# Fillers for TensorE, two products on VectorE and a new work list in a fused recurrence and highway kernel

## The chip, the cores and the metric

The kernel runs on one core of one Trainium2 chip. The metric is device time in microseconds (us), the median over several executions. Five executions of the kernel before gave 213.85, 214.18, 214.79, 215.29 and 215.34 us: median 214.79. One execution was taken with the hardware profiler; all durations below come from it.

## What is computed

Inputs are `x` and `f_logit` (4 sequences, 6336 steps, 256 channels, fp32), a `lower_bound` per channel, and two 256x256 weights with a bias. First a gated recurrence along each sequence, then a highway layer on its output:

```python
sig = 1.0 / (1.0 + np.exp(-f_logit))
f = lower_bound + (1.0 - lower_bound) * sig
h = f[:, t] * h + (1.0 - f[:, t]) * x[:, t]        # for each t; y[:, t] = h
H = np.maximum(y @ w_h, 0.0)
T = 1.0 / (1.0 + np.exp(-(y @ w_t + b_t)))
out = T * H + (1.0 - T) * y                        # 25344 tokens x 256, fp32
```

## The kernel before

**Units and pieces.** Work is cut into 25 units. A full unit is 1024 tokens of one sequence, as 8 blocks of 128 tokens; the last unit holds the remaining 192 tokens of each of the four sequences. The recurrence side (the "front") takes a unit in one piece, except the first three, which are cut so that work can begin on small loads: unit 0 gives pieces 0, 1 and 2 (2, 2 and 4 blocks), unit 1 pieces 3 and 4, unit 2 pieces 5 and 6 (4 blocks each). From piece 7 on a piece is mostly a whole unit. The highway side (the "back") takes whole units, except the last.

**One piece, step by step.** Each step has a letter, by which the work list names it.
- L and X: SP loads `f_logit` (tile `lt`) and `x` (tile `xt`), each with 5 buffers (line 106).
- U: ScalarE makes the gate u = sigmoid(-f_logit) in fp16 (L154).
- P: a product bv = u * x in bf16, one operation for two blocks of tokens (128x512), on GpSimd (L160). A piece of 2 blocks has one product, of 4 two, of 8 four.
- A: TensorE transposes u, block by block, into PSUM as uT (L198); F: ScalarE turns uT into the decay f, one operation for each half of the channels (L205).
- B: TensorE transposes bv into PSUM as bT (L215). A and B share two PSUM slots, numbered 0 and 1; the digit behind A or B in the list is the slot.
- S: VectorE's scan along time, y = f * y + bT, one operation for each half of the channels (L230). The factor 1 - lower_bound is left out of y here and put into the weights and matrices behind it.
- Q and W: the two halves of the raw weights are loaded (L125), and VectorE makes the fp16 weights from them in two operations (L148). Each W needs both loads.
- Z and G: TensorE's matmuls on y for the gate (zp) and for the other branch (gp, with y already subtracted through the weights), four of 512 columns for each half of the channels (L245), in three PSUM slots 0 to 2 that O shares.
- T: ScalarE's sigmoid of zp (L251). D: VectorE's d = max(gp, -y') (L256), with y' = (1 - lower_bound) * y, the true recurrence output. E and H: e = d * t, on VectorE (L166), and in part on GpSimd (L160).
- O: TensorE adds y' and e while it transposes them back into token order, two matmuls for each half of the channels of a block (L296 and L297). C and V: ScalarE or VectorE copies the result out of PSUM (L303). R: SP stores it (L309).

**What sets the order.** All of it is written out by hand in one string, `PLAN`. The loop at L365 reads it letter by letter, gives each letter its next piece, and pins each instruction to that order. Each engine carries out its own letters strictly in this order and waits where an operand or a buffer is not ready; so what stands in the list behind a waiting instruction of the same engine waits too. SP issues loads and stores from one queue, in list order.

**VectorE beside GpSimd.** `vector_mul` (L165) records a VectorE product, and the next GpSimd product is made to wait for it (L158 to L163). This is used for e. `EARLY` (L69) lists products of u and x that would go to VectorE through letter p; it is empty.

Of the kernel before, what the change touches and what calls it, by code (L numbers as in the profile page):

```python
# [11 lines left out]
FP32 = mybir.dt.float32  # L12
BF16 = mybir.dt.bfloat16
# [6 lines left out]
def kernel(  # L20
# [16 lines left out]
    nc = tc.nc  # L37
    B, S, D = x.shape
    assert D == 256
    P = 128  # L40
    NH = D // P
    NB = 8
# [23 lines left out]

    LASTQ = 2

    EARLY = []  # L69

# [7 lines left out]
    singles = ctx.enter_context(tc.tile_pool(name="singles", bufs=1))  # L80
# [4 lines left out]
    def new(key, shape, dtype):  # L85
        return pools[key].tile([P, *shape], dtype, tag=key, name=key)

    def pin(ins):
        return tc.keep_in_program_order(ins)
# [12 lines left out]
    def load(i, name, src):  # L102
        u, j0, j1 = fronts[i]
        np_, j = units[u][0], run(fronts[i])
        t = fs[i][name] = new(name, [NB, D], FP32)
        pin(nc.sync.dma_start(t[:np_, :j1 - j0].rearrange("p (k j) d -> p k (j d)", j=j), tokens(src, u, j0, j1, j)))
# [6 lines left out]
    def shape(piece):  # L113

        u, j0, j1 = piece
        return units[u][0], j1 - j0

    lb = singles.tile([P, NH], FP32, name="lb")
    bt = singles.tile([P, NH], FP32, name="bt")
# [4 lines left out]
    def load_weights(k):  # L124
        pin(nc.sync.dma_start(w_raw[:, 1 - k], (moe_w_t, moe_w_h)[k].rearrange("(h p) o -> p h o", p=P)))  # L125
# [25 lines left out]
    def gate(i):  # L151
        np_, nb = shape(fronts[i])
        u = fs[i]["u"] = new("u", [NB, D], FP16)
        pin(nc.scalar.activation(u[:np_, :nb], fs[i]["lt"][:np_, :nb], AF.Sigmoid, scale=-1.0))  # L154
# [13 lines left out]
    def product(i, k, mul):  # L168
        np_, _ = shape(fronts[i])
        if "bv" not in fs[i]:  # L170
            fs[i]["bv"] = new("bv", [NB // 2, D, 2], BF16)
        mul(inner(fs[i]["bv"][:np_, k:k + 1])[:, 0], fs[i]["u"][:np_, 2 * k:2 * k + 2],
            fs[i]["xt"][:np_, 2 * k:2 * k + 2])
# [9 lines left out]
    def psum(slot, shape, key, dtype):  # L183
        tag = ("one" if dtype in (FP16, BF16) else "two") + slot
        return ps1.tile([P, *shape], dtype, tag=tag, name=key)
# [126 lines left out]
    def each(pieces, count):  # L312
        return [(i, k) for i, piece in enumerate(pieces) for k in range(count(piece))]

    def halves_of(pieces):
        return each(pieces, lambda p: len(halves(p)))
# [7 lines left out]
    kinds = {  # L324
        "L": (lambda i, _: load(i, "lt", f_logit), each(fronts, lambda p: 1)),
        "X": (lambda i, _: load(i, "xt", x), each(fronts, lambda p: 1)),
        "Q": (lambda i, k: load_weights(k), [(0, 0), (0, 1)]),
        "U": (lambda i, _: gate(i), each(fronts, lambda p: 1)),
        "P": (lambda i, k: product(i, k, gpsimd_mul), [p for p in products if p not in EARLY]),
        "p": (lambda i, k: product(i, k, vector_mul), [p for p in products if p in EARLY]),  # L330
        "A": (decay_pe, halves_of(fronts)),
        "F": (decay_act, each(fronts, lambda p: NH)),
# [14 lines left out]
    }  # L347

    PLAN = (
        "XLLLXXLXLQQUUA0A1PFFFUFUB0PSSB1A0FFPSSPB1A0XLLXLXXPFUFSSWWPB1A0G0Z1PFFUPSSDPXLLXLB0A1G2Z0PUTFFTPPB1S"  # L350
        "SDUSSEZ1A0G0G2A1DDPFTFFPPZ1A0B1O0O2PSSTFECCUB0Z1B1G0G2SDSDA0Z0TUFTPPPPPPA0G1B1FXLLLXRRXLXDESA0Z0Z2O1"
        "UFTCTB0G0A1O1O2SDPPPFCCB1A0Z1G0O2FTUCB0G1PPPHPSDSEDPA1Z0Z2B0O1FTUCTESA1G0G1B0DDHPPPPSZ2O0O1FUTCCB1SA"
        "0G2Z0B1FDUTPHPPSXXLRLRRRLRXLRRZ1A0G2O0PDTFCEEG1B1A0O2O0UFCCDSG1B0A1Z2Z0SDPHPPPPFTTA1B0O2O1G0HPSFCCZ2"
        "B1A0Z1DUTFTEG0O2PSPLXXRXRRRRDPPHCB1SA0O1G0Z2B1FCUTDEPSG1Z0A0O2FTCPDPPHB1A0Z1G0O2SFTCDEB0Z1A1G0PLLXRR"
        "RRSDPPPUFTO2B0A1Z0G1SHDCFTEO2B0G0Z1A1PPPPCUFTSDHO2B0A1G0Z1SCFTO2B0A1DEPSZ1G0PPPCUFTDHO2B0A1O0G1SCFCD"
        "EZ2B0A1Z0PSTFTPPPG1B1O2A0O0DUCFCSG1Z2A1B0HDELXLLRXRLLRXRRRRRXPSTFPPZ1G0O2B1DTCSZ1G2A0O0PHUFTCDEB1A0G"
        "2Z1O0PSPFTCDPPHB0G1G2A1Z0UFTSA0B1FDEDSPO1O0Z2B0PPCCTPHSO1A1G0Z2B0UFTCDEPSA1G0Z2O1PPDB0FTCSA1Z2G0O1PH"
        "FUCTDELXRRXXRRLRLXXRRRA1B0G0Z1PSFTO2DCB1A0G1Z0O2PPPHSUFCTDEB1A0Z1G2O0PSDFTCB0A1Z1G2SFPPPHDO0B1A0G2ET"
        "UCFPSO1PZ0CDTB1A0Z1G2SFTUHO0A0B1DFG1EPPPPSO2A0CCZ0DFB1O2Z1B0TCUTSESHPPG0A1Z2G1DDRRRRRRRRFFTA1B0O2Z0Z"
        "1FCFSEHTTG2B1G0O1RSDDCO2SRHCZ0G1STRO2TDDEZ0CTERTG1O2O0DVDVCO2CREVO1CRO0RCVRR"  # L360
    )
    assert all(PLAN.count(k) == len(places) for k, (_, places) in kinds.items())
    todo = {k: iter(places) for k, (_, places) in kinds.items()}
    letters = iter(PLAN)
    for k in letters:  # L365
        kinds[k][0](*next(todo[k]), *([next(letters)] if k in "ABZGO" else []))
# [1 line left out]
_INS = ['x', 'f_logit', 'lower_bound', 'moe_w_h', 'moe_w_t', 'moe_b_t']  # L368
# [26 lines left out]
```

## Time and profile before

| | us |
|---|---|
| median of five executions | 214.79 |
| the profiled execution, its own time | 214.18 |
| its span, first to last instruction | 212.3 |
| VectorE (DVE) busy | 195.3 (92%) |
| ScalarE (ACT) busy | 193.7 (91%) |
| TensorE matmuls (PE) busy, with waits inside the pipeline | 187.8 (88%) |
| GpSimd (POOL) busy | 160.9 (76%) |
| data moved by DMA | 78.68 MB, 371 GB/s over the span |

The profile is a page of summaries, and the trace behind it can be asked for stretches of time, for single tiles and for the waits of each engine. A row of a timeline gives start and duration in us, engine, source line, operation, what it writes and reads, its shape, and how many equal instructions follow each other; in brackets stands how long the engine was idle before and what ended that. A duration can overlap that of the next instruction, so a chain is best read from start to start. "Busy" of an engine is an average over stages with different limits: here the ramp at the start, the long middle and the tail must be read apart.

### The profile page before, as it was taken

The page shows a single profiled execution, that of the slowest core. Times are in us where ns is not written, and L with a number is a line of the kernel's source. Part 1 is how long each engine was busy: PE and PEld are TensorE (multiplying, and loading weights), DVE is VectorE, ACT ScalarE, POOL GpSimd, SP SyncE. Part 2 cuts the span into 40 slices and gives each one's busy share as a digit, 9 for nine tenths or more (in the row PEclk, how much of TensorE's full clock was granted, in tenths as well). Part 3 has the DMA queues.
Part 4 walks back from the last instruction along what each step waited for, and adds up shares of the span by engine and source line. Part 5 has one row for each costly group of instructions (what it writes and reads, how often), then busy time and mean ns, then how long its engine had stood idle before and what let it go on. Part 6 is the DMA issues. An engine that isn't in the chain of part 4 may idle for free.

```text
span 212.3 us, 4616 instructions
## 1 busy us (share of the span) xinstructions
PE 187.8 (88%) x1800; PEld 131.3 (62%) x1800; DVE 195.3 (92%) x154; ACT 193.7 (91%) x194; POOL 160.9 (76%) x133
## 2 busy tenths in 40 slices
PE   0368998899898999999999999999999999999970
PEld 0255564577575757666767666668576676866770
DVE  1269999999999999999999999999999999999980
ACT  2757999999999999999999999999999999998760
POOL 4485756979599698978988898898899876866400
PEclk9999999999999999999999999999999999999999
DMA  4999999999999999999999999999999996252465
GB/s 96 392 414 426 428 429 421 429 420 420 429 421 424 421 424 421 425 424 418 431 417 421 428 431 420 419 414 431 414 429 412 357 406 269 98 201 99 198 259 188
DMA packets 17349, 78.68 MB, mean 371 GB/s; under 512 B 2352, under 2 KB 2864, under 8 KB 11952
## 3 DMA queue, kind: packets, MB, share of 16 engines
q1 hardware_dynamic: 16784, 78.39, 90.3%
q8 instruction: 14, 0.23, 0.4%
q10 hardware_dynamic: 544, 0.00, 0.1%
q14 instruction: 7, 0.06, 0.1%
HBM read 52.43 MB, written 25.95 MB: 369 GB/s over the span
## 4 chain that ended last, share of the span: by engine, by line
DMA 32%; PE 27%; ACT 21%; DVE 8%; issue 7%; POOL 1%; SPq 1%; ACTq 1%; DVEq 0%; POOLq 0%
DMA xt<-in_x_dram 12%; DMA lt<-in_f_logit_dram 12%; DMA out_dram<-o 8%; PE zp L245 8%; ACT t L251 7%; PE gp L245 6%; ACT u L154 5%; ACT f L205 5%; ACT o L303 4%; DVE d L256 4%; PE uT L198 4%; PE op L296 3%; PE op L297 3%; PE bT L215 3%; DVE y L230 3%
## 5 line engine op out<-in xcount | busy, mean ns | idle before, releaser
L160 POOL TENSOR_TENSOR bv<-u,xt 128x512 bf16<-128x512 f16 (+1 forms) x100 | 114.6, 1180 | 31.5 <-DVE e L166 14.1
L230 DVE TENSOR_TENSOR_SCAN y<-f,y,bT 128x1024 bf16<-128x1024 f16 (+3 forms) x56 | 106.3, 1916 | 2.1 <-PE bT L215 2.1
L205 ACT ACTIVATE f<-uT,ncc 128x1024 f16<-128x1024 f16 (+3 forms) x60 | 65.0, 1095 | 2.5 <-PE uT L198 2.5
L251 ACT ACTIVATE t<-zp,bt 128x1024 bf16<-128x1024 f32 (+1 forms) x52 | 62.9, 1228 | 0.3 <-DVE e L166 0.3
L256 DVE SCALAR_TENSOR_TENSOR d<-y,ncc,gp 128x1024 bf16<-128x1024 bf16 (+1 forms) x52 | 62.3, 1208 | 0.4 <-issue 0.2
L245 PEld LDWEIGHTS <-w_sb 128*128 128x128 f16 x400 | 37.8, 98 | 37.3 <-issue 5.7
L303 ACT COPY o<-op 128x1024 f32<-128x1024 f32 (+2 forms) x50 | 54.9, 1137 | 4.2 <-PE op L297 2.1
L154 ACT ACTIVATE u<-lt 128x2048 f16<-128x2048 f32 (+3 forms) x30 | 52.7, 1759 | 5.1 <-DMA lt<-in_f_logit_dram 5.1
L245 PE MATMUL gp<-y,w_sb 128*128 128x512 bf16 (+1 forms) x200 | 51.4, 382 | 0.7 <-ACT t L251 0.4
L245 PE MATMUL zp<-y,w_sb 128*128 128x512 bf16 (+1 forms) x200 | 50.6, 377 | 0.9 <-DVE d L256 0.6
L296 PE MATMUL op<-diag,y 128*128 128x128 f16 (+1 forms) x400 | 49.2, 219 | 1.8 <-DVE d L256 0.7
L160 POOL TENSOR_TENSOR e<-d,t 128x1024 bf16<-128x1024 bf16 x21 | 44.8, 2135 | 7.3 <-DVE e L166 2.6
L297 PE MATMUL op<-ident_b,e 128*128 128x128 bf16 (+1 forms) x400 | 49.2, 219 | 0.0
L297 PEld LDWEIGHTS <-e 128*128 128x128 bf16 (+1 forms) x400 | 44.7, 114 | 5.5 <-issue 3.3
L296 PEld LDWEIGHTS <-y 128*128 128x128 bf16 (+1 forms) x400 | 44.8, 114 | 2.7
L198 PE MATMUL uT<-ident_h,u 128*128 128x128 f16 (+1 forms) x400 | 32.1, 226 | 9.9 <-ACT u L154 7.4
L198 PEld LDWEIGHTS <-u 128*128 128x128 f16 (+1 forms) x400 | 27.3, 101 | 17.1 <-ACT u L154 7.6
L215 PE MATMUL bT<-ident_f,bv 128*128 128x128 f32 (+1 forms) x200 | 32.5, 284 | 5.2 <-DVE y L230 2.4
L215 PEld LDWEIGHTS bT<-ident_f,bv 128*128 128x128 f32 (+1 forms) x200 | 22.8, 145 | 12.1 <-issue 4.1
L166 DVE TENSOR_TENSOR e<-d,t 128x1024 bf16<-128x1024 bf16 (+2 forms) x26 | 18.9, 734 | 0.1
L230 DVE TENSOR_TENSOR_SCAN y<-f,bT 128x512 bf16<-128x512 f16 (+2 forms) x8 | 10.4, 1335 | 3.9 <-PE bT L215 3.9
L135 DVE TENSOR_SCALAR cc<-lb 128x2 f32<-128x2 f32 x1 | 0.2, 170 | 4.5 <-DMA lb<-in_lower_bound_dram 4.5
(19 smaller groups left out, 10.9 us busy)
## 6 DMA issues: line engine op xcount, KB each, us to landing
out_dram<-o SPq DMA_DIRECT2D x48, 512.0 KB, 13.6
lt<-in_f_logit_dram SPq DMA_DIRECT2D x21, 1024.0 KB, 14.7
xt<-in_x_dram SPq DMA_DIRECT2D x21, 1024.0 KB, 15.8
lt<-in_f_logit_dram SPq DMA_DIRECT2D x5, 512.0 KB, 8.1
xt<-in_x_dram SPq DMA_DIRECT2D x5, 512.0 KB, 8.2
lt<-in_f_logit_dram SPq DMA_DIRECT2D x2, 384.0 KB, 13.0
xt<-in_x_dram SPq DMA_DIRECT2D x2, 384.0 KB, 11.3
xt<-in_x_dram SPq DMA_DIRECT2D x2, 256.0 KB, 5.1
```

The source lines that it names most:

```text
L154: pin(nc.scalar.activation(u[:np_, :nb], fs[i]["lt"][:np_, :nb], AF.Sigmoid, scale=-1.0))
L160: ins = pin(nc.gpsimd.tensor_mul(out_, a, b))
L198: pin(nc.tensor.transpose(uT[:, j * np_:(j + 1) * np_], fs[i]["u"][:np_, j, h * P:(h + 1) * P], ident_h[:np_, :np_]))
L205: pin(nc.scalar.activation(f[:, :N].rearrange("p (k q j) -> p k q j", q=np_, j=j), fs[i]["uT", h].rearrange("p (k j q) -> p k q j", q=np_, ...
L215: pin(nc.tensor.transpose(t[:, k // r, k % r], fs[i]["bv"][:np_, k, h * P:(h + 1) * P].rearrange("p d j -> p (d j)").bitcast(FP32), ident_ ...
L230: pin(nc.vector.tensor_tensor_scan(y, fs[i]["f", h][:, c:c + w], fs[i]["bT", h][:, c:c + w], 0.0 if prev is None else prev, op0=ALU.mult, ...
L245: pin(nc.tensor.matmul(p[:, a:e], w_sb[:, k, ki, h * P:(h + 1) * P], y_of(j)[:, ki, a:e], start=ki == 0, stop=ki == NH - 1))
L251: pin(nc.scalar.activation(bs[j]["t"][:, m, :width(backs[j])], bs[j]["zp", m], AF.Sigmoid, bias=bt[:, m:m + 1]))
L256: pin(nc.vector.scalar_tensor_tensor(bs[j]["d"][:, m, :width(backs[j])], y_of(j)[:, m], ncc[:, m:m + 1], bs[j]["gp", m], op0=ALU.mult, op1 ...
L296: pin(nc.tensor.matmul(o, y[:, h, cols], diag[:, h], start=True, stop=False))
L297: pin(nc.tensor.matmul(o, bs[j]["e"][:, h, cols], ident_b, start=False, stop=True))
L303: pin(copy(bs[j]["o", q][:np_, a:e], bs[j]["op", q][:np_, a:e]))
```

## The change

Three things change.

1. A tile `filler` of zeros is made by VectorE at the very start, and a letter M is added: one TensorE matmul of 512 columns of these zeros with themselves, into a PSUM tile `busy` in slot 2 that nobody reads. The new list has 20 of them: nine ahead of the first transposes, one between the transposes of pieces 0 and 1, one ahead of piece 0's B, seven behind it and ahead of piece 2's A, one ahead of piece 1's B and one ahead of piece 2's.
2. `EARLY` names the product of piece 0 and the first of piece 2's two. VectorE makes these (letter p): the first ahead of all scans, the second between the scans of piece 0's two halves. GpSimd makes two products fewer.
3. `PLAN` is another list. Its ramp loads f_logit of pieces 0 and 1 first, then x of both, f_logit and x of piece 2, one half of the weights, f_logit and x of piece 3, the other half of the weights, and f_logit of piece 4; before it was x of piece 0, f_logit of 0, 1 and 2, x of 1 and 2, f_logit and x of 3, f_logit of 4, and both weight halves. VectorE's order in the ramp was S S S S S S W W S S D S S D and is p S p S S S S W S W S S D D S S. Later on the letters are the same in number, and many neighbours and slots are exchanged.

```diff
-    EARLY = []
+    EARLY = [(0, 0), (2, 0)]
...
+    filler = singles.tile([P, 512], BF16, name="filler")
+    nc.vector.memset(filler, 0.0)
...
     PLAN = (
-        "XLLLXXLXLQQUUA0A1PFFFUFUB0PSSB1A0FFPSSPB1A0XLLXLXXPFUFSSWWPB1A0G0Z1PFFUPSSDPXLLXLB0A1G2Z0PUTFFTPPB1S"
-        "SDUSSEZ1A0G0G2A1DDPFTFFPPZ1A0B1O0O2PSSTFECCUB0Z1B1G0G2SDSDA0Z0TUFTPPPPPPA0G1B1FXLLLXRRXLXDESA0Z0Z2O1"
...
+        "LLXXLXQLXUUMMMMMMMMMA0MA1pFFFUFMB0PSpSMMMMMMMA1MB0FFUSSPMB1A0QLLXLXLXXPFFUSWSWPB0A1Z0G1PUFUFTPSSDPLL"
+        "XXLG2B0A1Z1PFFTPPB1DSSUSSEZ2A0G0G1A1DDPFTFFPPZ2B0A1O0O1PSSTFCUCEB1Z2G0B0G1SDSDA1Z0UTFTPPPPPPA1G2B0FX"
...
     )
...
+    busy = psum("2", [NB * P], "busy", FP32)
     letters = iter(PLAN)
     for k in letters:
+        if k == "M":
+            pin(nc.tensor.matmul(busy[:, :512], filler[:, :P], filler, start=True, stop=True))
+            continue
         kinds[k][0](*next(todo[k]), *([next(letters)] if k in "ABZGO" else []))
```

More of the change, by code (lines that the diff above doesn't have):

```diff
@@ L349 @@
     PLAN = (
-        "XLLLXXLXLQQUUA0A1PFFFUFUB0PSSB1A0FFPSSPB1A0XLLXLXXPFUFSSWWPB1A0G0Z1PFFUPSSDPXLLXLB0A1G2Z0PUTFFTPPB1S"
-        "SDUSSEZ1A0G0G2A1DDPFTFFPPZ1A0B1O0O2PSSTFECCUB0Z1B1G0G2SDSDA0Z0TUFTPPPPPPA0G1B1FXLLLXRRXLXDESA0Z0Z2O1"
-        "UFTCTB0G0A1O1O2SDPPPFCCB1A0Z1G0O2FTUCB0G1PPPHPSDSEDPA1Z0Z2B0O1FTUCTESA1G0G1B0DDHPPPPSZ2O0O1FUTCCB1SA"
-        "0G2Z0B1FDUTPHPPSXXLRLRRRLRXLRRZ1A0G2O0PDTFCEEG1B1A0O2O0UFCCDSG1B0A1Z2Z0SDPHPPPPFTTA1B0O2O1G0HPSFCCZ2"
-        "B1A0Z1DUTFTEG0O2PSPLXXRXRRRRDPPHCB1SA0O1G0Z2B1FCUTDEPSG1Z0A0O2FTCPDPPHB1A0Z1G0O2SFTCDEB0Z1A1G0PLLXRR"
@@ L355 @@
[L355 to L359, printed above, removed]
@@ L360 @@
-        "1FCFSEHTTG2B1G0O1RSDDCO2SRHCZ0G1STRO2TDDEZ0CTERTG1O2O0DVDVCO2CREVO1CRO0RCVRR"
+        "LLXXLXQLXUUMMMMMMMMMA0MA1pFFFUFMB0PSpSMMMMMMMA1MB0FFUSSPMB1A0QLLXLXLXXPFFUSWSWPB0A1Z0G1PUFUFTPSSDPLL"
+        "XXLG2B0A1Z1PFFTPPB1DSSUSSEZ2A0G0G1A1DDPFTFFPPZ2B0A1O0O1PSSTFCUCEB1Z2G0B0G1SDSDA1Z0UTFTPPPPPPA1G2B0FX"
+        "RLLXLLRXXDESA1Z0Z1O2UFTCTB1G0A0O2O1SDPPPFCCB0A1Z2G0O1FTUCB1G2PPHPPSDSEDPA0Z0Z1B1O2FTTUCESG0A0G1B1DDH"
+        "PPPPPSO2O0Z1FUCTCB0SA1G2Z1B0FDUTHPPSLLRRRRRXXXRRLLLZ0G2A1O1PDTFCEEG0B0O2A1O1UFCCDSG0B1A0Z2Z1SDHPPPPP"
@@ new lines @@
+        "FTTB0A1O2O0G1HPSFCCB1Z2Z0A0DUTFTEG1O2PSPRXDPPHCB1SA0Z0G1O2B1FUTCDEPSA0G1Z0O2FTCPDPPHB1A0Z1G0O2SFTCDE"
+        "B0A1Z1G0O2PXRXRRRLRXXRLRRSDPPPUFTB0A1Z0G1SHDCFTEO2B1Z0G1A0PPPPCUFTSDHO2B1A0Z1G0SCFTO2B1A0DEPSZ1G0PPP"
+        "CFTUDHB0O2O1A1G0SCFCDEZ2B0A1Z1PSTFTPPG0O2A1B0O1DCFCUSG2Z0Z1B1A0PHDELLRRRLXXRLXRRLRRPSTFPPG2O0A0B1DTF"
+        "CUSO1G2Z0PHCTDEA0B1Z2G1O0PSPFTCDPPHB0A1Z2G1FTUSG0B1A0FDEDSPO2O1Z0B0PPCCTPHSO2A1G1Z0B0UFCTDEPSA1Z1G2O"
+        "0PPPDB0TFCSZ1A1G2O0HUFCTDERXXRRRRRLLXXRLRXB0A1Z2G0PSFTO1DCB1A0O2G0Z1PPPHSUFTCDEB1A0Z0G1O2PSDFTCB0A1G"
@@ L361 @@
+        "0SFPPHDO1B1A0Z2G0EUCTFPPSO1PZ2CDTB0A1Z1G0SFTUHO2A1B0DFG1EPPPPSO0A1CCZ2DFB0Z0O1B1TUCTSESHPPG2A0Z1G0DD"
+        "RRRRRRRRFFTB0A1O1Z2Z0FFCSEHTTG1G2B1O0RSDDCO1SRHCZ2G0STRO1TDDEZ2CTERTG0O1O2DCVDO1CVREVO0CRO2RCVRR"
     )
+    assert set(PLAN) <= {*kinds, *"M012"}
     assert all(PLAN.count(k) == len(places) for k, (_, places) in kinds.items())
     todo = {k: iter(places) for k, (_, places) in kinds.items()}
+    busy = psum("2", [NB * P], "busy", FP32)
     letters = iter(PLAN)
     for k in letters:
+        if k == "M":
+            pin(nc.tensor.matmul(busy[:, :512], filler[:, :P], filler, start=True, stop=True))
+            continue
```

## The prediction

> **What bounds the kernel now.** I read the page's busy times first, then the busy time by stretches, then the stretch before full load instruction by instruction.
>
> ```profile
> PE 187.8 (88%) x1800; PEld 131.3 (62%) x1800; DVE 195.3 (92%) x154; ACT 193.7 (91%) x194; POOL 160.9 (76%) x133
> ```
>
> Two engines are almost full. The stretches (start:end, length, then PE, PEld, DVE, ACT, POOL busy, clock, DMA share, GB/s) show that they are full from about 15 us to 190 us and that only the two ends have room:
>
> ```profile
> 10.00:15.00 5.00, 3.63 (x22) 2.77 (x22) 3.18 (x5) 2.63 (x5) 4.68 (x5) 1.00 1.04 410
> 15.00:20.00 5.00, 3.39 (x16) 2.31 (x17) 5.00 (x6) 3.62 (x6) 3.11 (x3) 1.00 1.04 425
> 80.00:100.00 20.00, 19.48 (x194) 13.71 (x192) 19.73 (x15) 20.00 (x20) 17.33 (x14) 1.00 1.01 422
> 100.00:120.00 20.00, 19.45 (x202) 13.98 (x199) 20.00 (x13) 20.00 (x19) 18.37 (x15) 1.00 1.02 424
> ```
>
> So the end of the kernel is set by how far VectorE has come when it becomes full, plus what it loses later. Later losses are small: 40 to 140 us show 19.90, 19.74, 19.73, 20.00 and 19.92 of 20, together 0.7 us. The chain that ended last names loads over its first 70 us; but from 15 us on no wait for a load holds VectorE or ScalarE, so I read those shares as DMA being busy alongside. VectorE's own timeline in the ramp:
>
> ```profile
> 9.53 1.26 DVE L230 TENSOR_TENSOR_SCAN y<-f,bT 128x256 bf16<-128x256 f16 x2 [3.92 <-PE bT L215]
> 11.30 1.39 DVE L230 TENSOR_TENSOR_SCAN y<-f,y,bT 128x256 bf16<-128x256 f16 x2 [0.50 <-PE bT L215]
> 14.01 2.45 DVE L230 TENSOR_TENSOR_SCAN y<-f,y,bT 128x512 bf16<-128x512 f16 x2 [1.32 <-PE bT L215]
> 16.38 2.30 DVE L148 SCALAR_TENSOR_TENSOR w_sb<-o,cc 128x512 f16<-128x512 f32 x2
> 18.60 2.32 DVE L230 TENSOR_TENSOR_SCAN y<-f,bT 128x512 bf16<-128x512 f16 x2
> 20.84 1.25 DVE L256 SCALAR_TENSOR_TENSOR d<-y,ncc,gp 128x1024 bf16<-128x1024 bf16 x1
> ```
>
> The number to beat is 18.60, the start of piece 3's scans: the work ahead of it is the same scans and weights in both kernels (plus two products after), and the work behind it is the same set too. GpSimd paces what feeds it:
>
> ```profile
> 9.29 3.57 POOL L160 TENSOR_TENSOR bv<-u,xt 128x512 bf16<-128x512 f16 x3 [1.40 <-DMA xt<-in_x_dram]
> ```
>
> Three products at 1.19 end at 12.86; then come 1.08 us of transposes (L215 at 12.83), then the scan at 14.01. TensorE's own timeline shows its clock:
>
> ```profile
> 18.34 1.91 PE L245 MATMUL gp<-y,w_sb 128*128 128x512 bf16 x4
> 20.05 1.13 PE L245 MATMUL zp<-y,w_sb 128*128 128x512 bf16 x4
> 21.89 1.03 PE L245 MATMUL gp<-y,w_sb 128*128 128x512 bf16 x4
> ```
>
> The next group starts 1.71 us after the first of these, and 0.87 us after the last (22.76): 427 against 217 ns a matmul. TensorE runs at half rate until about 20 us, whatever the clock column says.
>
> **The skill.** The Trainium skill's "TensorE: Matmul & The Clock Gate", section "What's actually happening", says that the array starts at half clock and is released by a busy window of some 3.4 us that runs free of the kernel. The trace agrees: the rate doubles after TensorE was gapless from 16.6 to 20 us, and not after the half-busy stretch before. Section "HAM oscillation" of that page puts the way back at idle gaps of some 3 us; here the half-busy last stretch (5.80 of 7 us, 200 to 207) kept full rate. No page says whether zeros count as work. "GPSIMD Engine Reference", section "Specifications", says that GpSimd shares its SBUF interface with VectorE operations of two SBUF inputs. The trace agrees: the weight operations take 0.73 us alone and 1.65 us beside a product.
>
> **The change, part by part.**
>
> *The nine leading fillers.* They wait only for a fill of zeros on VectorE, which idles until 4.52 us. At 427 ns they take 3.84 us, from about 1.2 to 5.0; the first real transposes wait for a gate that cannot end before 5.0 (below). Cost 0 under that cover; without it up to 0.4.
>
> *The eleven later fillers.* At full clock 0.22 us each. The seven (1.5 us) stand ahead of piece 2's transposes, which wait anyway for ScalarE's last operation on piece 1 at about 10.7; at half clock they would end at 11.7. The gapless stretch 1.2 to 6.0 holds a whole window in about (4.8-3.4)/3.4 = 4 of 10 phases, somewhat more if nine tenths busy is enough; otherwise the next candidate ends by 10 to 12. So full clock by 12 at the latest, if zeros count.
>
> *Loads.* The data order decides the ramp. Landings before, by MiB queued so far: 0.25 at 4.3, 0.5 at 6.0, 0.75 at 7.3, 1.25 at 8.5, 1.5 at 9.2, 2.0 at 10.4, 2.5 at 11.7, 3.0 at 12.9, 3.5 at 14.2, 4.0 at 15.5, 4.5 at 16.8, 5.0 at 18.0, 5.5 at 19.3 (issue time plus time to landing; DMA is at 0.97 to 1.05 throughout). I keep this table. New order: f_logit 0 at 4.3, 1 at 6.0, x 0 at 7.3, x 1 near 8.0, f_logit 2 at 9.2, x 2 at 10.4, a weight half at 11.0, f_logit 3 at 12.3, x 3 at 13.5, the other weight half at 14.2, f_logit 4 at 15.5, 5 at 16.8, x 4 at 18.0, f_logit 6 at 19.3. Everything is on SP's one queue, no store is passed in the ramp, and x 4 comes 1.2 us later than before.
>
> *The VectorE products.* The trace has none. "VectorE: DVE Perf Modes", errata section, gives (N+151)/0.96 for an fp32 two-tensor operation: 0.69 us at N=512 (estimate); the nearest row, the uncontended weight operation of the same size, is 0.73. Upper end 1.65, as beside GpSimd. I take 0.7: GpSimd's next product is made to wait for it.
>
> *Now the path.* Product 0 at 7.3 to 8.0 (x 0); transposes 0.4; first scan near 8.5 to 9.1, 1 us earlier than before. But VectorE then stands at the second product, which needs x 2: 10.4 to 11.1. Behind it in VectorE's queue waits the scan of piece 0's other half, ready since 9; behind that, PSUM for piece 1's bT. Scan 11.1 to 11.75; bT of piece 1 takes about 0.45; piece 1's scans 12.2 to 13.55 (0.60+0.66 spacing). GpSimd's other product of piece 2 runs 11.15 to 12.35, its transposes 12.45 to 13.0 at full clock, so they are not waited for. Piece 2's scans 2 x 1.13 and the weights (0.64 and 1.58, one of them beside GpSimd's products of piece 3, as before) give 13.55 + 2.26 + 2.22 = 18.05 for piece 3's scans, against 18.60: gain 0.55. The second weight half (14.2) is needed at 14.7. Ends: product at 1.2 or more, 18.55 or later and no gain; weights without collision, 17.1.
>
> *After it.* The new list makes two d in a row behind piece 3's scans, so gp is needed at 20.3 and 21.5. At full clock zp, gp, gp of 0.87 each from 18.1 end at 19.0, 20.0 (with latency) and 20.9: no wait. Piece 4: x 4 at 18.0, products to 20.4, bT at 21.3; its scan is due at 22.65. ScalarE reaches the first t near 20.9, held by f_logit 6 at 19.3, against 21.63: it gains 0.7, so it does not take the gain back. The loads to 42 us land with 1.4 to 2.0 us to spare for the gates, later mostly 5 or more, so an advance of 0.5 is covered.
>
> *The redrawn list.* Same counts of everything else on every engine; pairs of zp, gp and bT swap slots and order. I cost it at 0, covered by full DVE and ACT queues, with -0.7 to +2 us as ends: at most the 0.7 of middle idle can vanish, and each late f or gp costs what it lacks.
>
> Sum: profiled span 212.3 - 0.55 = 211.75; the execution took 214.18, so 1.9 lie around the span: 213.6. That run is 0.6 below the median of 214.79; on the median: **214.2 us**.
>
> **Rivals.**
>
> *Slower by the clock:* zeros do not count, or the thin stretch from 13 to 18 us (some 35 to 48% busy) lets the clock fall. It decides if matmuls are at half rate after 11.7 us. Then the seven fillers end at 11.7, piece 2's transposes 12.8, piece 1's bT 13.5, piece 3's scans at 19.5 (+0.95), and zp, gp at 1.71 each from 19.6 make the first d wait for gp until 23.0 instead of 21.8 (+1.2): 214.8 + 2.1 = 216.9. For: no evidence on zeros. Against: the last stretch kept its clock.
>
> *Slower by the list:* both full engines have no slack to absorb one late input per unit. For: four small VectorE losses before, 0.2 to 0.35 us each, show that it is tight. Ten more make +2 to +3: about 217.
>
> *No gain:* x 2 binds both kernels (10.4), and a contended product eats the rest: 214.8.
>
> *Faster:* ramp 0.55, middle 0.7, tail waits for op (0.6): 214.8 - 1.85 = 212.9.
>
> **How the numbers follow.** Forecast 0.40, its own range 213.8 to 214.7; no gain 0.12; faster rival 0.20; clock 0.10; list 0.18. Half a per cent, about what this kernel's runs can tell, is 1.07 us: under 213.7 is faster, over 215.9 slower. The faster rival and the forecast's low edge give 0.22; clock, list and a few from no gain 0.30; the rest 0.48. The range 212.9 to 216.7 leaves one in ten on each side.
>
> **What would show it.** Right: fillers before 5 us; 217 ns matmuls before 12 us; a VectorE product that waits for x near 10.4; piece 3's scans at 17.9 to 18.3; gapless VectorE after it. Wrong: 427 ns later than 12 us; a wait of d for gp near 20; idle VectorE in the middle over 1 us; weights waited for at 14; a product over 1 us.

## The result and the profile after

The changed kernel takes 215.23 us (median of 39 executions, 213.25 to 216.48); the kernel before, run beside it on the same chips, takes 214.34 (76 executions, 213.41 to 215.70). The ratio, of fast executions only (the longest, 216.48, is more than 1.5% above the shortest and counts as slow), is 1.0027, with a 95% interval of 1.0015 to 1.0039; the plain quotient of the two medians is 1.0042. So it is slower by 0.3 to 0.4%, inside the half per cent that the prediction called no change, and on the other side of its forecast. The profiled execution took 214.57 us, against 214.18 before.

The head of the page, its line of busy times, its clock row and one of its costliest groups:

```profile
span 212.8 us, 4650 instructions
...
PE 192.6 (90%) x1820; PEld 132.0 (62%) x1820; DVE 197.0 (93%) x157; ACT 194.2 (91%) x194; POOL 158.4 (74%) x131
...
PEclk9996999999999999999999999999999999999998
...
L373 PE MATMUL busy<-filler 128*128 128x512 bf16 x20 | 7.5, 504 | 1.2 <-DVE filler L120 1.2
```

TensorE has 20 instructions more, the fillers. VectorE has three more (a fill of zeros and two products) and GpSimd two fewer. The clock row is the first clue: full almost from the start, with one slice at 6. Busy time by stretches of the changed kernel (columns as before: start:end, length, PE, PEld, DVE, ACT, POOL busy, clock, DMA share, GB/s):

```profile
10.00:15.00 5.00, 2.66 (x24) 1.62 (x23) 4.41 (x6) 3.22 (x5) 3.08 (x3) 1.00 1.03 414
15.00:20.00 5.00, 3.47 (x17) 2.06 (x18) 4.99 (x5) 3.99 (x6) 2.76 (x3) 0.72 1.04 427
20.00:25.00 5.00, 4.46 (x30) 2.58 (x29) 3.81 (x4) 3.54 (x5) 3.58 (x4) 0.94 1.02 428
80.00:100.00 20.00, 19.38 (x201) 13.98 (x200) 19.75 (x15) 20.00 (x20) 17.52 (x13) 1.00 1.01 423
```

VectorE is fuller than before from 10 to 20 us (9.40 us of 10, against 8.18), and loses 1.19 us of the next five. The middle is as before. VectorE's timeline in the ramp says where:

```profile
6.74 0.74 DVE L170 TENSOR_TENSOR bv<-u,xt 128x512 bf16<-128x512 f16 x1 [1.24 <-DMA xt<-in_x_dram]
...
9.92 0.74 DVE L170 TENSOR_TENSOR bv<-u,xt 128x512 bf16<-128x512 f16 x1 [1.09 <-DMA xt<-in_x_dram]
10.55 0.67 DVE L234 TENSOR_TENSOR_SCAN y<-f,bT 128x256 bf16<-128x256 f16 x1
11.81 2.56 DVE L234 TENSOR_TENSOR_SCAN y<-f,y,bT 128x256 bf16<-128x256 f16 x3 [0.59 <-PE bT L219]
14.29 1.63 DVE L152 SCALAR_TENSOR_TENSOR w_sb<-o,cc 128x512 f16<-128x512 f32 x1
15.83 1.27 DVE L234 TENSOR_TENSOR_SCAN y<-f,y,bT 128x512 bf16<-128x512 f16 x1
17.02 0.72 DVE L152 SCALAR_TENSOR_TENSOR w_sb<-o,cc 128x512 f16<-128x512 f32 x1
17.67 2.32 DVE L234 TENSOR_TENSOR_SCAN y<-f,bT 128x512 bf16<-128x512 f16 x2
21.19 2.47 DVE L260 SCALAR_TENSOR_TENSOR d<-y,ncc,gp 128x1024 bf16<-128x1024 bf16 x2 [1.20 <-PE gp L249]
```

Piece 3's scans start at 17.67, 0.93 earlier than the 18.60 before. Right behind them VectorE stands idle for 1.20 us, because the first d waits for gp. TensorE's timeline of the changed kernel at that place:

```profile
13.35 0.61 PE L202 MATMUL uT<-ident_h,u 128*128 128x128 f16 x8 [0.74 <-DVE y L234]
15.36 0.63 PE L219 MATMUL bT<-ident_f,bv 128*128 128x128 f32 x4 [1.40 <-ACT f L209]
17.16 1.01 PE L202 MATMUL uT<-ident_h,u 128*128 128x128 f16 x8 [1.17 <-DVE y L234]
17.96 1.91 PE L249 MATMUL zp<-y,w_sb 128*128 128x512 bf16 x4
19.67 2.34 PE L249 MATMUL gp<-y,w_sb 128*128 128x512 bf16 x8
```

Eight transposes take 0.61 us at 13.35 and 1.01 at 17.16. From zp's start to gp's is 1.71 us, 427 ns a matmul: half rate again. The clock records of the trace give full rate from 6.92 to 17.16 us, half until 20.57, and full from there on. So the fillers did bring full clock early, but in the stretch between the fillers and the first real matmuls it was lost again, and came back only after that work.

At the next scan that both lists have in the same place (piece 5's first), VectorE stands at 25.94 against 25.55: the gain of 0.93 has become a loss of 0.39. The middle adds 0.1: the last scan is 0.49 late. The last copies lose more. Two rows of VectorE's timeline at the end, of the changed kernel and then of the one before:

```profile
203.94 0.69 DVE L307 COPY o<-op 128x512 f32<-128x512 f32 x1 [0.82 <-ACT o L307]
...
207.35 0.69 DVE L307 COPY o<-op 96x512 f32<-96x512 f32 x1 [0.54 <-PE op L301]
```

```profile
202.84 0.69 DVE L303 COPY o<-op 128x512 f32<-128x512 f32 x1 [0.20 <-PE op L297]
...
206.25 0.69 DVE L303 COPY o<-op 96x512 f32<-96x512 f32 x1 [0.27 <-PE op L297]
```

The last copy ends at 208.04 against 206.94, 1.1 us late where the scan was 0.49 late. In the new list ScalarE's copy (C) of one PSUM tile stands ahead of VectorE's (V): DVDVCO2C has become DCVDO1CV. The two copies run one after the other: ScalarE's of 203.32 to 203.91, then VectorE's at 203.94, after a wait of 0.82 us. The tile's last matmul ends near 203.3, so about 0.6 of the wait is ScalarE's copy. In the old order it is ScalarE that waits for VectorE. Not all of this reaches the time: the span ends 4.75 us behind the last copy here and 5.38 before, and so only 0.48 later (212.79 against 212.32).

The profiled execution is not the commonest. Of the 40 executions, 23 had a mean TensorE clock of 0.975 to 0.977 over their span (median 215.45 us), 14 had 0.988 to 0.990 as the profiled one (median 214.44), two had 0.983, and one had 0.995 (213.25, the shortest). By groups the time follows how long the clock was low; for a single execution the mean says less, as it also holds the half rate after the last matmuls (from 211.72 us in the profile).

### The profile page after: what moved, and what is told of

Its sections match the earlier page's. It is cut to its first block, busy times and chain, and to the rows that moved or that the text cites. A ratio compares the mean times of both kernels' runs of the same rounds, so it can differ in the third digit from the quotient of the medians.

```text
span 212.8 us, 4650 instructions
## 1 busy us (share of the span) xinstructions
PE 192.6 (90%) x1820; PEld 132.0 (62%) x1820; DVE 197.0 (93%) x157; ACT 194.2 (91%) x194; POOL 158.4 (74%) x131
## 4 chain that ended last, share of the span: by engine, by line
PE 42%; ACT 26%; DVE 13%; issue 12%; DMA 3%; SPq 1%; DVEq 0%; ACTq 0%
PE zp L249 12%; PE gp L249 10%; ACT f L209 8%; ACT t L255 7%; PE uT L202 6%; ACT u L158 6%; DVE d L260 5%; ACT o L307 5%; DVE y L234 5%; PE bT L219 5%; PE op L301 5%; PE op L300 4%; DMA xt<-in_x_dram 3%; DVE e L170 1%; SPq L106 1%
## 5 line engine op out<-in xcount | busy, mean ns | idle before, releaser
L164 POOL TENSOR_TENSOR bv<-u,xt 128x512 bf16<-128x512 f16 (+1 forms) x98 | 112.0, 1177 | 32.8 <-DVE e L170 15.8
L249 PE MATMUL zp<-y,w_sb 128*128 128x512 bf16 (+1 forms) x200 | 51.2, 381 | 2.0 <-DVE d L260 1.0
L249 PE MATMUL gp<-y,w_sb 128*128 128x512 bf16 (+1 forms) x200 | 50.8, 379 | 0.3
L202 PE MATMUL uT<-ident_h,u 128*128 128x128 f16 (+1 forms) x400 | 31.2, 222 | 5.2 <-DVE y L234 2.7
L219 PE MATMUL bT<-ident_f,bv 128*128 128x128 f32 (+1 forms) x200 | 31.2, 276 | 3.9 <-ACT f L209 1.9
L202 PEld LDWEIGHTS <-u 128*128 128x128 f16 (+1 forms) x400 | 26.6, 99 | 12.7 <-issue 6.1
L219 PEld LDWEIGHTS bT<-ident_f,bv 128*128 128x128 f32 (+1 forms) x200 | 22.1, 141 | 12.6 <-issue 4.9
L373 PE MATMUL busy<-filler 128*128 128x512 bf16 x20 | 7.5, 504 | 1.2 <-DVE filler L120 1.2
```

The costliest lines, as they stand in the source:

```text
L164: ins = pin(nc.gpsimd.tensor_mul(out_, a, b))
L202: pin(nc.tensor.transpose(uT[:, j * np_:(j + 1) * np_], fs[i]["u"][:np_, j, h * P:(h + 1) * P], ident_h[:np_, :np_]))
L219: pin(nc.tensor.transpose(t[:, k // r, k % r], fs[i]["bv"][:np_, k, h * P:(h + 1) * P].rearrange("p d j -> p (d j)").bitcast(FP32), ident_ ...
L249: pin(nc.tensor.matmul(p[:, a:e], w_sb[:, k, ki, h * P:(h + 1) * P], y_of(j)[:, ki, a:e], start=ki == 0, stop=ki == NH - 1))
```

## The experiments

The theory (the clock): after the fillers TensorE is too idle, its clock falls back, and the first zp and gp come at half rate to a VectorE that needs them early. Rivals: the list (late neighbours all over the middle), the tail's order of copies, and the products on VectorE. All ratios are to the kernel before, run beside, with a 95% interval.

**The changed kernel again**, unchanged, to see whether another execution shows the same place.

> The changed kernel once more, beside the others. Its executions on record fall into groups by granted clock: 14 of 40 near 0.989 with a median of 214.4 us, 23 near 0.976 with 215.5. Clock theory: the same two groups again, and where this profile falls into the lower clock, TensorE is at half rate for two or more windows of 3.4 us between 12 and 24 us and the first d waits for gp by more than the 1.2 us of the profile on record. List theory (the redrawn list is at fault, the clock only rides along): the time does not go with the clock. Ratio to before 1.002 to 1.004 by both.

215.18 us, ratio 1.005 (1.003 to 1.007), mean clock 0.976. VectorE's and TensorE's rows:

```profile
21.67 2.53 DVE L260 SCALAR_TENSOR_TENSOR d<-y,ncc,gp 128x1024 bf16<-128x1024 bf16 x2 [1.63 <-PE gp L249]
```

```profile
15.40 1.05 PE L219 MATMUL bT<-ident_f,bv 128*128 128x128 f32 x4 [1.40 <-ACT f L209]
...
18.02 1.91 PE L249 MATMUL zp<-y,w_sb 128*128 128x512 bf16 x4
19.72 3.16 PE L249 MATMUL gp<-y,w_sb 128*128 128x512 bf16 x8
```

Here the clock fell at 15.46 and returned at 22.28, two steps of 3.41 us instead of one. More of gp runs at half rate, d waits 1.63 and the last scan is 1.03 late. This is the commoner form.

**More fillers in the thin stretch** (hold): 14 matmuls on zeros more, between 12.5 and 17.3 us; nothing else is changed.

```diff
-  ..SSPMB1A0QLLXLXLXXPFFUSWSWPB0A1Z0G1..
+  ..SSPMB1MMMA0MMMMMMQLLXLXLXXPFFUSWSWPB0MMMMMA1Z0G1..
```

> The changed kernel with 14 more fillers in the thin stretch: 3 ahead of the transposes of piece 3, 6 behind them, 5 ahead of those of piece 4. At full clock they take 0.65, 1.3 and 1.1 us and fit into gaps of 0.75, 1.4 and 1.2 us. Clock theory: granted clock 0.995 or more in nearly every execution, the first d no longer waits for gp, VectorE is 1.2 us earlier than in the profile on record, time 213.0 to 213.9, ratio to before 0.994 to 0.998. List theory: clock high, but the time stays within 0.4 us of the changed kernel, because another input is late next; ratio 1.001 to 1.004.

213.32 us (213.16 to 214.02), ratio 0.9971 (0.9959 to 0.9982): 1.9 us less than the changed kernel's median, and faster than before. TensorE's and VectorE's timelines:

```profile
13.91 1.46 PE L374 MATMUL busy<-filler 128*128 128x512 bf16 x6
15.48 0.63 PE L219 MATMUL bT<-ident_f,bv 128*128 128x128 f32 x4
15.94 1.24 PE L374 MATMUL busy<-filler 128*128 128x512 bf16 x5
17.27 0.61 PE L202 MATMUL uT<-ident_h,u 128*128 128x128 f16 x8
17.72 1.03 PE L249 MATMUL zp<-y,w_sb 128*128 128x512 bf16 x4
18.58 1.89 PE L249 MATMUL gp<-y,w_sb 128*128 128x512 bf16 x8
```

```profile
17.79 2.32 DVE L234 TENSOR_TENSOR_SCAN y<-f,bT 128x512 bf16<-128x512 f16 x2
20.03 2.44 DVE L260 SCALAR_TENSOR_TENSOR d<-y,ncc,gp 128x1024 bf16<-128x1024 bf16 x2
```

zp takes 0.86 us from start to start, d does not wait, and the last scan is 0.76 earlier than before. Piece 3's scans start no earlier than in the changed kernel (17.79 against 17.67): all of the gain is the wait that is gone. Since all else in the list, the tail and the products included, is as it was, this settles the main cause.

**The first two groups in the other order** (gfirst): gp ahead of zp, so that the first d finds its gp at half clock too.

```diff
-  ..PB0A1Z0G1PUFUF..
+  ..PB0A1G1Z0PUFUF..
```

> The changed kernel with one exchange: piece 3 and 4's first gp stands ahead of the first zp on TensorE (G1 Z0 in place of Z0 G1), no further fillers. Where the clock has fallen back, the first d gets its gp 1.7 us earlier and waits for nothing, but the second d needs the second gp, which still ends last of the three groups near 22 us. Clock theory: the wait moves to the second d, gain 0.0 to 0.4 us on the changed kernel (median 214.8 to 215.4). Order theory (zp ahead of gp is the fault): 0.9 to 1.3 us faster, 214.0 to 214.3.

214.95 us, ratio 1.0031 (1.0015 to 1.0047). VectorE's rows:

```profile
20.04 1.28 DVE L260 SCALAR_TENSOR_TENSOR d<-y,ncc,gp 128x1024 bf16<-128x1024 bf16 x1
...
22.78 1.28 DVE L260 SCALAR_TENSOR_TENSOR d<-y,ncc,gp 128x1024 bf16<-128x1024 bf16 x1 [1.46 <-PE gp L249]
```

The first d is on time, and the second waits 1.46 us for the other gp. The wait belongs to the rate at which TensorE delivers zp, gp, gp, not to one place in the list.

**Without the fillers** (nofill): the new list, loads and products, all 20 M left out.

> The changed kernel with none of its 20 fillers. Clock theory: half rate until about 21 us as in the kernel before; zp before gp at 1.71 us each keeps the first d waiting to about 21.5 us, so 215.0 to 216.0, ratio 1.003 to 1.008: the fillers buy little as they stand. If the fillers were worth what they are for, it would be slower than the changed kernel by 1 us or more (ratio over 1.008). If they only cost, it is faster than before (ratio under 1.000).

215.27 us, ratio 1.0063 (1.0045 to 1.0080). One of VectorE's waits (what waits and for what: us in all, times, longest):

```profile
DVE d L260 <- PE gp L249: 1.6, 1, 1.6
```

d waits 1.6 us, as in the commoner form of the changed kernel. The last scan is 1.20 late; in the changed kernel it was 0.49 and 1.03. So the 20 fillers as they stand bought next to nothing, and without a held clock the new list costs about one us against the old one.

**The tail's old order of copies** (tail): the letters that copy the last results of the full units are put back as they stood before.

```diff
-  ..O1O2DCVDO1CVREV..
+  ..O1O2DVDVCO1CREV..
```

> The changed kernel with one exchange at the end of the list: the last but two output groups are copied in the order of the kernel before (VectorE's copy of both groups ahead of ScalarE's), in place of ScalarE first. In the profile on record VectorE waits 0.82 us there for ScalarE's copy of the same group, and 0.54 us more for the last; before it waited 0.2, 0.17 and 0.27. Tail theory: the wait goes, 0.4 to 0.7 us faster than the changed kernel, ratio to before 1.000 or less. Rival: the end hangs on the last stores (4.8 us behind the last copy, against 5.2 before), and the copies' 0.6 us buys 0.2 us or less.

214.66 us, ratio 1.0032 (1.0013 to 1.0051); VectorE's copies wait 0.20, 0.17 and 0.28 us, as before. The time alone says little, since this kernel's clock falls back too, for a varying stretch. So the same edit was made where the clock is held.

**Held clock and the old tail** (holdtail): the edits of hold and tail together.

> The changed kernel with the 14 further fillers of the run hold and with the tail's copies in the order of the kernel before. The clock is steady there, so the tail can be priced alone. In the trace of hold VectorE still waits 0.82 and 0.54 us at the copies. Tail theory: last copy 0.5 us earlier, 212.8 to 213.0, ratio to before 0.994 to 0.996. Rival (the last stores decide): within 0.2 us of hold (213.3).

212.95 us (212.82 to 214.11), ratio 0.9956 (0.9943 to 0.9969), 0.37 less than hold. The last copies of hold, then of holdtail:

```profile
202.69 0.69 DVE L307 COPY o<-op 128x512 f32<-128x512 f32 x1 [0.82 <-ACT o L307]
...
206.10 0.69 DVE L307 COPY o<-op 96x512 f32<-96x512 f32 x1 [0.54 <-PE op L301]
```

```profile
202.06 0.69 DVE L307 COPY o<-op 128x512 f32<-128x512 f32 x1 [0.20 <-PE op L301]
...
205.47 0.69 DVE L307 COPY o<-op 96x512 f32<-96x512 f32 x1 [0.27 <-PE op L301]
```

The copy's wait goes from 0.82 us (for ScalarE) to 0.20, the last copy comes 0.63 earlier, the profiled span ends 0.34 earlier and the median is 0.37 lower. That is about the price of this one place in the redrawn list; against the kernel before, run beside each, it is 0.3 (the two intervals overlap).

**Six of the fourteen** (hold6): only the fillers behind piece 3's first transposes.

```diff
-  ..SSPMB1A0QLL..
+  ..SSPMB1A0MMMMMMQLL..
```

> The changed kernel with only 6 of the 14 further fillers, those behind piece 3's transposes (14.0 to 15.3 us). Clock theory with a bound between 25 and 47% busy per window (one of 25% fell back, one of 47% did not): every window from 12 to 18 us then holds over 45% work, so the clock stays in nearly every execution: 213.2 to 213.6, one group of times. If the bound lies higher, some executions fall back: two groups, the upper at 214.4 to 215.5.

213.28 us (213.15 to 213.73), ratio 0.9958 (0.9943 to 0.9973), the same as hold. Six fillers in the one window that was too thin are enough. In its profile the clock did fall back once, but earlier, from 7.7 to 11.1 us. VectorE's first weight operation:

```profile
15.26 0.79 DVE L152 SCALAR_TENSOR_TENSOR w_sb<-o,cc 128x512 f16<-128x512 f32 x1
```

Piece 2's first scan comes at 14.06, 0.82 later than in hold (in part because x landed later). The weight operation behind it then takes 0.79 us, where in hold it took 1.62 beside a GpSimd product; here it is GpSimd whose two products take longer (2.73 us against 2.28). So piece 3's scans start at 17.80 all the same. This fall cost nothing because a collision happened to go the other way, and not because an early fall is harmless: in holdpool below the like costs a wait of 0.84 us.

**Without the nine leading fillers** (nolead): hold, less the nine M at the start.

```diff
-  LLXXLXQLXUUMMMMMMMMMA0MA1p..
+  LLXXLXQLXUUA0MA1p..
```

> The changed kernel with the 14 further fillers but without the nine leading ones. Clock theory: half rate until a window from about 8 to 12 us is three quarters busy, full clock from there; piece 2's transposes at half rate cost at most 0.5 us on the way to piece 3's scans, of which the collision of a weight operation with GpSimd hides a part: within 0.4 us of hold (213.2 to 213.7). Rival: the leading fillers are what brings the gain, so that it is near the run nofill (215.3).

214.54 us, ratio 1.0025 (1.0011 to 1.0038): 1.2 over hold, three times the most I had expected. TensorE's and VectorE's rows:

```profile
8.60 3.19 PE L374 MATMUL busy<-filler 128*128 128x512 bf16 x7
11.59 1.06 PE L202 MATMUL uT<-ident_h,u 128*128 128x128 f16 x8
```

```profile
18.49 2.32 DVE L234 TENSOR_TENSOR_SCAN y<-f,bT 128x512 bf16<-128x512 f16 x2
21.65 2.47 DVE L260 SCALAR_TENSOR_TENSOR d<-y,ncc,gp 128x1024 bf16<-128x1024 bf16 x2 [0.84 <-PE gp L249]
```

Full clock comes only at 13.22 us. Until then the seven fillers that stand ahead of piece 2's transposes run at 427 ns and take 3 us instead of 1.5, and what is behind them in TensorE's order is late: piece 3's scans by 0.70 against hold, and then d waits 0.84 us for gp, though the clock is full by then. The later fillers were cheap here only because the clock was full when they ran; the leading nine, in dead time, made it so.

**Fillers alone** (beforefill): the old list, its loads and products, with 32 fillers put in so that the clock is held through the ramp.

```diff
-  XLLLXXLXLQQUUA0A1PFFFUFUB0PSSB1A0FFPSSPB1A0XLL..
+  XLLLXXLXLQQUU(M x11)A0MMA1MPFFFUFUB0MMMMPSSB1A0(M x6)FFPSSPB1A0(M x8)XLL..
```

> The list of the kernel before, with its own products and loads, and 32 fillers in its gaps on TensorE: 11 ahead of the first transposes, 2, 1 and 4 among the next ones, 6 ahead of the B of piece 2 and 8 ahead of that of piece 3. Clock theory: full clock from about 6 to 10 us on; piece 2's transposes take 0.6 in place of 1.08 us, its scans start near 13.5 in place of 14.0, piece 3's near 18.1 in place of 18.6: 213.5 to 214.0, ratio to before 0.996 to 0.999. Rival: the gain of hold comes from the new load order and the moved products, so that fillers in the old list give nothing (ratio 0.999 to 1.002) or cost where they stand ahead of real work.

213.40 us, ratio 0.9970 (0.9957 to 0.9984), the same as hold. VectorE's and GpSimd's rows:

```profile
15.35 1.39 DVE L152 SCALAR_TENSOR_TENSOR w_sb<-o,cc 128x512 f16<-128x512 f32 x2
16.65 2.33 DVE L234 TENSOR_TENSOR_SCAN y<-f,bT 128x512 bf16<-128x512 f16 x2
...
25.84 1.59 DVE L170 TENSOR_TENSOR e<-d,t 128x2048 bf16<-128x2048 bf16 x1
...
32.19 1.85 DVE L170 TENSOR_TENSOR e<-d,t 128x2048 bf16<-128x2048 bf16 x1
```

```profile
25.19 7.77 POOL L164 TENSOR_TENSOR bv<-u,xt 128x512 bf16<-128x512 f16 x6 [2.81 <-DMA xt<-in_x_dram]
```

Piece 3's scans start at 16.65, 1.95 earlier than before. Three things make that up. The two weight operations take 1.30 us up to the scans, against 2.22, since a GpSimd product holds up neither now: 0.92. From the end of piece 2's products to its first scan (12.98) it is 0.70 us, against 1.15, with the transposes at full rate: 0.45. And those products themselves end 0.58 earlier, in step with loads that landed earlier in this execution (f_logit of piece 1 at 6.71 us against 7.31), which the edit doesn't touch. Of the 1.95, 1.1 is given back by the 15th scan (0.84 ahead, and 0.92 at the last). Piece 6's x is there only at 25.19, though VectorE is ahead (24.38 before); GpSimd's products of it now run beside the two e of VectorE, which take 1.59 and 1.85 us where they took 1.19 and 1.23. Fillers alone thus give what the whole change with a held clock gives; the new list and the VectorE products were not needed for that much.

**The products back on GpSimd** (holdpool): hold with both early products on GpSimd.

```diff
-    EARLY = [(0, 0), (2, 0)]
+    EARLY = []
-  ..A1pFFFUFMB0PSpS..
+  ..A1PFFFUFMB0PSPS..
```

> The changed kernel with the 14 further fillers and with both products back on GpSimd (EARLY empty). Both kernels wait for x of piece 2 at about 9.9 us. Worked from the trace of hold: GpSimd makes products 0, 1, 2, 3 by 7.9, 9.1, 11.1 and 12.25 us, piece 2's transposes end near 12.9 and its scan starts near 13.0, against 13.2 with the products on VectorE, where the second product and the scan behind it stand in VectorE's own way. Theory: the products are worth nothing at full clock; within 0.3 us of hold (213.1 to 213.5). Rival: they are worth their 1.2 us on GpSimd each, so that it is slower than hold by 0.6 us or more.

213.36 us over all, ratio 0.9977 (0.9959 to 0.9995), but in two groups: 13 of 22 executions at 212.94 to 213.48, the others at 213.7 to 215.3. Its profile is of the second group: clock lost from 7.9 to 11.3 us, VectorE waits 2.46 us for bT of piece 1. Piece 3's scans still start at 17.86; what is lost is 0.84 us that d then waits for gp. The first group, about 0.2 below hold, suggests that the VectorE products bring nothing at full clock; their group alone was not profiled, so that is not shown here.

**Everything that helped together** (best): hold, the old tail, the products on GpSimd, and four more fillers in all: five more around piece 1's transposes, where the clock was lost in holdpool, and one fewer ahead of piece 0's B.

```diff
-  ..A0MA1pFFFUFMB0PSpS..
+  ..A0MMMA1MMMPFFFUFB0PSPS..
```

> The changed kernel with the 14 further fillers, the tail's copies as in the kernel before, both products back on GpSimd, and the fillers near 5 to 8 us raised from 3 to 6 (3 before and 3 behind the transposes of piece 1). In the run holdpool the lower 13 of 22 executions lay at 212.9 to 213.5 and the others 1 us higher, with a window of 33% work at 4.5 to 7.9 us that cost the clock. Clock theory: no window under 45% is left, one group of times; with the tail's 0.37 us, 212.5 to 212.8, ratio to before 0.992 to 0.995. If the products are worth something on VectorE after all, it is not faster than holdtail (212.95).

212.81 us (212.69 to 213.90), ratio 0.9946 (0.9926 to 0.9967): 1.3 us of median below the kernel before, run beside it (214.10), and 2.4 below the changed kernel. It can't be told apart from holdtail (212.95). VectorE's rows:

```profile
16.60 2.32 DVE L234 TENSOR_TENSOR_SCAN y<-f,bT 128x512 bf16<-128x512 f16 x2
19.77 2.47 DVE L260 SCALAR_TENSOR_TENSOR d<-y,ncc,gp 128x1024 bf16<-128x1024 bf16 x2 [0.85 <-PE gp L249]
```

The ramp is now as short as in beforefill, again with two weight operations of 0.72 us, and d waits again, though the clock is full: in this list zp stands behind a transpose of bv that waits for a GpSimd product until 15.93, then five fillers and eight transposes, and starts at 17.84. Moving Z0 and G1 forward may help here; that was not tried.

## Why the prediction was wrong

**The bound: right.** The end follows how far VectorE has come when it is full. From the 12th scan to the last, the lead or lag to the kernel before changes by 0.12 us in the changed kernel (+0.37 to +0.49), by 0.05 in hold (-0.81 to -0.76), by 0.05 in best (-1.05 to -1.10). It was carried to the end as said, the tail apart.

**Loads and products: right; that it came out better than forecast is mostly luck.** The first product on VectorE waited for x until 6.74, not 7.3; the second until 9.92, not 10.4. Each took 0.74 us, 0.63 from start to start; I had taken 0.7. No collision there, as GpSimd was made to wait. Piece 1's scans started at 11.81 (forecast 12.2), the weights took 1.54 and 0.65 from start to start (1.58 and 0.64), and piece 3's scans came at 17.67 instead of 18.05. The forecast gain of 0.55 was 0.93. The forecast's table of landings was read from a single execution, and landings vary: with the same order of loads the second product found its x at 9.92 us here, at 10.39 in hold6 and at 10.43 in nolead. And the forecast's own sum is about 0.1 too late: 12.2 + 0.60 + 0.66 is 13.46, and with 2.26 and 2.22 that makes 17.94, not 18.05. The Trainium skill's estimate of the product ("VectorE: DVE Perf Modes", errata section), 0.69, lies between the two readings of 0.74 and 0.63.

**The fillers' own cost and the first release: right.** They ended by 5.2 us, zeros counted as work, and full clock came at 6.9, before the 12 us given as the latest.

**The step that failed: "At full clock zp, gp, gp of 0.87 each from 18.1 end at 19.0, 20.0 and 20.9: no wait."** They took 1.71 us for zp alone, and d waited 1.2 us, 1.6 in the commoner form. hold, where the three do run at 0.86, has no wait and is 1.9 us faster. The kernel before had half rate until 20.24 us and no such wait: its list puts gp first and asks for one d there, the next at 24.37. The new list asks for two d in a row behind zp, gp, gp, and so needs the full rate that the old one could do without; nofill, the new list at half rate, has the wait too (1.6 us). The mechanism stood in the prediction as a rival (the thin stretch lets the clock fall), with 1 chance in 10; its 2.1 us were 0.95 for late scans of piece 3, which did not come about, and 1.2 for the wait of d, which did. That it came to the tenth in the profiled execution is chance (1.63 in again).

Two readings behind that 1 in 10 were wrong. First, the stretch from 13 to 18 us was called 35 to 48% busy. The last window of it before the clock fell, 13.75 to 17.16 us, shows 0.83 us of PE busy in 3.41 (24%), and busy times contain waits inside the pipeline. The array's own time is columns times 0.42 ns (217 ns for 512, gapless). That window holds four fp32 transposes of 0.11 us and about one fp16 transpose of 0.055: 0.5 of 3.41 us, 14%. Second, the old kernel's last stretch was taken as proof that half busy keeps the clock. It was not half busy but a dense part and a thin one: by the same measure its last window, 204.6 to 208.0, holds 25 matmuls of 128 columns and the end of another, about 40%. It was evidence about 40%, and I used it for 14%. The Trainium skill ("TensorE: Matmul & The Clock Gate", section "HAM oscillation") puts the way back at idle gaps of more than about 3.4 us. Here it fell with no gap that long: the longest two around it were 1.40 and 1.17 us, by the timeline above. The measurement decides.

**The second step that failed: "The redrawn list. I cost it at 0."** In the middle that held (0.1 us). In the tail the order of two copies costs some 0.3 to 0.4 us, shown by holdtail against hold. And the order zp, gp, gp with two d behind it, part of the same list, is what the fallen clock hits. The faster rival had counted on the tail to gain 0.6.

**The rest of the list: not fully settled.** With the clock held, the new list with the old tail (212.95) and the old list with fillers (213.40) differ by 0.45 us, on one chip (ratios 0.9956 and 0.9970, whose intervals overlap). Which of loads, products and order makes it, if it is real, was not told apart.

## What to carry to other kernels

Dummy matmuls have to hold the clock all the way to the first dense real work, not only raise it: count the columns that the array takes (not its busy time) in every window of 3.4 us from the first filler on, and fill the thin ones; here six matmuls were worth 1.9 us. In the runs here the leading fillers were free, as they ran in dead time, and later ones were cheap at full rate and delayed what stood behind them at half rate. An advance can be given back, or a delay hidden, by a collision of VectorE with GpSimd that comes, goes or changes its loser (0.9 us for one weight operation here), so look at what the shifted engine will then run beside. And a profile is one execution: the same load landed at 9.92 us in one and at 10.43 in another.

## What the runs showed of the hardware

**Where the clock falls and rises.** In every trace the changes of clock lie on a grid of 3.41 us, whose phase differs from execution to execution. Taking each window's array time as above (at half rate 0.83 ns a column; fp32 transposes count double: 0.11 against 0.055 us in hold), full rate was lost in the ramps after windows filled to 14% (the changed kernel), 25 (tail), 26 (again), 33 (gfirst and holdpool) and 35 (hold6), at the ends of the kernels after 0 to 24%, and kept after all of 40% or more (40, 42, 42, 44, 44 and 45 are the thinnest). Half rate was left after windows filled to 79% and more, and not after 72, 70, 68, 61 or 54%. At half rate a column takes twice the time, so the two bounds, counted in columns, are one. In all 13 traces a window with at most about 2,980 columns was followed by half rate and one with at least about 3,260 by full rate, whichever rate it ran at; where between the two the bound lies is not shown. Matmuls on zeros count as work: with nine or more of them ahead, full rate came at 4.3 to 6.9 us, and without at 13.2 (nolead), 20.2 (before) and 22.2 (nofill).

**One program, several times.** Since the grid's phase is free, a thin stretch of the length of a window or two is caught whole in some executions and in others not. This fits the spread of the changed kernel over 213.25 to 216.48, with the clock to match, while hold and hold6, without such a stretch ahead of zp, stay within 0.9 and 0.6 us; it was traced in single executions only (17.16 to 20.57 us at half rate in one, 15.46 to 22.28 in the other).

**VectorE beside GpSimd.** The weight operation (512 columns, fp32) took 0.72 us alone and 1.63 beside a GpSimd product (both in the changed kernel), and e (2048 columns, bf16) 1.19 alone and 1.59 to 1.85 beside. Which of the two is held up changes with small shifts: in hold the weight operation took 1.62 us and GpSimd's two products of that time 2.28, in hold6 0.79 and 2.73.
